# Three pairs of banks for h, one addition per operand, and other places for two sums in an attention and FFN kernel

## The chip, the cores and the metric

The kernel runs on one core of a Trainium2 chip. The metric is the device time of one execution in microseconds (us), from its start to its end. Three executions of the kernel before gave 823.32, 825.64 and 825.73 us, median 825.64. The profile was taken from an execution of 825.11 us.

## The reference

Attention within chunks of 64 tokens, then a feed-forward network with a quadratic activation. B is 8, H is 8, S is 576, D is 64, so x has 4608 rows of 512.

```python
# q, k, v: [B, H, S, D], cut into chunks of 64 along S
scores = scale * q_c @ k_c.transpose(-1, -2)
attn = exp(scores - max); attn = attn / (sum + 1e-9)
x = (attn @ v_c).reshape(...)            # 4608 x 512
h = x @ w_in                             # w_in 512 x 2048
g = where(h >= 1, h, where(h <= -1, 0, (h + 1) ** 2 / 4))
out = g @ w_out                          # w_out 2048 x 512
```

## The kernel before

**Tiles.** The 4608 tokens are nine tiles of 512. Tiles 0 to 2 go through the two products of the network directly: `ffn_in` (products on line 607) and `ffn_out` (line 643). Each float32 product is made of three, of a rounded high part and a low rest. Tiles 3 and 4, 5 and 6, 7 and 8 are three pairs, and a pair is treated together by the Strassen-Winograd scheme: seven products of combined blocks where eight would do it plainly. They are called pair 3, pair 5 and pair 7 here, by their first tile (the loop variable `t`).

**h of a pair.** The hidden dimension of a pair is cut into eight blocks, p = 0 to 7, and each block has seven products P1 to P7 (`product`, matmuls on line 899, six of 128x512 per product). P3(2) stands for product P3 of block 2. A block uses one pair of banks of the accumulation memory. Its first bank takes P1, P6, P5 and P3 one after the other, each added to what is there, and its second bank takes P2, then P7, then P4. Between the products the other engines read the bank. ACT and DVE are the scalar and the vector engine:

- after P1, ACT copies the bank to a snapshot ("note a", line 724); after P2, DVE adds bank and snapshot to h (line 920) and the activation follows (ACT lines 926 and 929, DVE line 930);
- after P6, ACT copies the bank to the other snapshot ("note u"); after P5, ACT copies it to h ("note h1") and DVE adds the bank of P7 to that ("add h1");
- P3 is activated straight from the bank (ACT line 926 and DVE line 930 read it); after P4, DVE adds the second snapshot ("add u") and the activation follows.

So P6 waits for note a, P5 for note u, P3 for note h1, P7 for the addition after P2, P4 for add h1, and the first product of a later block on the same banks waits for the activation of P3. The order of the products is `alternating`: block p and block p-1 are interleaved, so that between two products on one bank there stand products on others. In pairs 3 and 5 a burst of attention work (32 small products on lines 487 and 465, then maxima, eight exponentials on line 530 and transposes) is put in after every ninth product; pair 7 has none.

**Banks.** There are four sets. `h_banks` are two tiles of one bank each (ps_h in the trace, ps_h_141 and ps_h_142 in the program). `o_banks[:2]` are two tiles of one bank each (ps_o_139 and ps_o_140). `o_banks[2:]` are the two halves of ONE tile of two banks, made by `bank_pair("ps_o23")` (ps_o_137). `ps_a` serves the attention. In the trace ps_o stands for all three ps_o tiles. The framework puts the waits into the program: it follows readers and writers tile by tile.

**Out of a pair.** `both_out` makes the seven products of g with w_out, over all eight blocks (line 1114). Its `operand_of` splits the operands into high and low parts, and the table `after` says at which product the operand blocks are added in place by DVE.

**The order.** A planner (`Plan`) records every operation with a cost and what it reads and writes, and emits them engine by engine, each when its inputs are ready by the plan's own times, by its place in the code less a head start `ahead` (LATER is -60, that is later). The plan knows the two halves of `o_banks[2:]` as two banks.

**Sums and stores.** `keep_factor` (line 957) copies blocks of w_out to DRAM for the pairs: eight of P1 in tile 0, sixteen of P2 and P4 in tile 1. `combine_out` (DVE line 728, then four stores) makes sums of w_out, eight of them, the last two, 6 and 7, in pair 3 at P1(1) and P1(4). They work in one of two sets of temporaries: `tmp` (which tile 2's output also uses on its way to DRAM) or the `alt` tiles, chosen by `again`.

Of the kernel before, what the change touches and what calls it, by code (L numbers as in the profile page):

```python
# [12 lines left out]
ALU = mybir.AluOpType  # L13
# [120 lines left out]
def kernel(  # L134
# [36 lines left out]
    ALONE = 2  # L171
# [12 lines left out]
    def buffers(pool, name, n, dtype=F32):  # L184
        return [
            (f"{name}{i}", pool.tile([P, T], dtype, name=f"{name}{i}", tag=f"{name}{i}"))
            for i in range(n)
        ]
# [32 lines left out]
    o_banks = buffers(psum, "ps_o", 2) + [(f"ps_o{2 + b}", o_pair[:, b, :]) for b in range(2)]  # L221
    h_banks = buffers(psum, "ps_h", 2)
# [492 lines left out]
    def cols(n):  # L715
        return slice(n * QC, (n + 1) * QC)
# [5 lines left out]
    def act_copy(cost, out, src, reads, writes, ahead=0):  # L722
        plan.add(
            "act", cost, lambda: nc.scalar.copy(out=out(), in_=src()), reads, writes, ahead=ahead  # L724
        )

    def dve(cost, op, out, one, two, reads, writes, ahead=0):
        plan.add("dve", cost, lambda: nc.vector.tensor_tensor(  # L728
            out=out(), in0=one(), in1=two(), op=op
        ), reads, writes, port=True, ahead=ahead)  # L730

    def part(ap, n):
        return lambda: ap()[:, cols(n)]

    def plain(ap):
        return lambda: ap().bitcast(F32)
# [45 lines left out]
    def rounded(ap):  # L782
        return lambda: ap().bitcast(F32R)

    def stage_of(again):
        if again:
            some = [(f"alt{n}_{i}", part_of(f"alt{n}", i)) for n in range(2) for i in range(2)]
            return *some, [lambda n=n: held[f"alt{n}"] for n in range(2)]
        return *((key, fixed(ap)) for key, ap in tmp_bufs), [fixed(pair) for pair in tmp_pairs]
# [162 lines left out]
    def keep_factor(name, p):  # L952
        n, half = RAW[name]
        j = 2 * p + n

        def send():
            nc.gpsimd.dma_start(  # L957
                out=sums[name, p].bitcast(F32), in_=weight["wo", j][:, :, cols(half)].bitcast(F32)
            )

        plan.add("pool", 0.7, send, (f"wo{j}_0", f"wo{j}_1"), (f"sums_{name}_{p}",), lag=3.0,
                 moving=0.8, ahead=LATER)

    def combine_out(p, again=False):
        js = (2 * p, 2 * p + 1)
        keys = [[f"wo{j}_{n}" for n in range(2)] for j in js]
        (k1, w1), (k12, s12), (k2, w2), (k34, s34), pairs = stage_of(again)
        for j, ks, key, w in zip(js, keys, (k1, k2), (w1, w2)):
            dve(0.6, ALU.add, w, lambda j=j: weight["wo", j][:, 0, :].bitcast(F32),
                lambda j=j: weight["wo", j][:, 1, :].bitcast(F32), ks, (key,), ahead=LATER)  # L970
        a11, a21, a12, a22 = (part(w, n) for w in (w1, w2) for n in range(2))
        s1, s2, s3, s4 = (part(w, n) for w in (s12, s34) for n in range(2))
        dve(0.34, ALU.add, s1, a21, a22, (k1, k2), (k12,), ahead=LATER)
        dve(0.34, ALU.subtract, s2, s1, a11, (k1,), (k12,), ahead=LATER)
        dve(0.34, ALU.subtract, s3, a11, a21, (k1,), (k34,), ahead=LATER)
        dve(0.34, ALU.subtract, s4, a12, s2, (k2, k12), (k34,), ahead=LATER)
        for hkey, hi, key, ap in ((k1, w1, k12, s12), (k2, w2, k34, s34)):
            act_copy(0.52, rounded(hi), ap, (key,), (hkey,), ahead=LATER)
            dve(0.6, ALU.subtract, rounded(ap), ap, hi, (hkey,), (key,), ahead=LATER)
        for n, name in enumerate(SUMS):  # L980
            def send(n=n, name=name):
                nc.gpsimd.dma_start(
                    out=sums[name, p].bitcast(F32), in_=pairs[n // 2]()[:, :, cols(n % 2)]
                )

            plan.add("pool", 0.7, send, ((k1, k12), (k2, k34))[n // 2], (f"sums_{name}_{p}",),
                     lag=3.0, moving=0.8, ahead=LATER)

    def whole_last(p, name, banks):
        got = product(p, name, banks)  # L990
        if name == "P1":
            note(snap("a"), got)
        elif name == "P2":
            add(whole_h(0), got, snap("a"))
            activate(whole_h(0), blocks["eA", p])
        elif name == "P6":
            note(snap("u"), got)
        elif name == "P5":
            note(whole_h(1), got)
            add(whole_h(1), kept[p], whole_h(1))  # L1000
            activate(whole_h(1), blocks["oB", p])
        elif name == "P7":
            kept[p] = got
        elif name == "P3":
            activate(got, blocks["eB", p])
            (k1, a1), (k2, a2) = blocks["oB", p], blocks["eB", p]
            dve(0.6, ALU.subtract, lambda: now(a2), lambda: now(a1), lambda: now(a2), (k1,), (k2,))
        else:
            add(whole_h(0), got, snap("u"))
            activate(whole_h(0), blocks["oA", p])  # L1010
# [46 lines left out]
    def both_out(t, wide=(), then=None):  # L1057
# [9 lines left out]
        if not last:  # L1067
# [2 lines left out]
        alone = ("P1", "P2", "P7", "P5", "P3")  # L1070
        sources = {"P1": "eA", "P2": "oA", "P6": "eA", "P7": "eB", "P4": "oA", "P5": "eA", "P3": "oB"}
        after = {
            "P1": ((ALU.add, "eB", "eA", "eA"),),
            "P6": ((ALU.subtract, "oA", "eA", "oA"), (ALU.subtract, "oB", "eA", "eA")),
        }
        at = dict(blocks)

# [4 lines left out]
        def operand_of(name, p):  # L1082
            raws = {n: (at[n, p][0], lambda n=n: now(at[n, p][1])) for n in ("eA", "oA", "eB", "oB")}
            slot = both(f"x{one_of('slots', some.get(name, every))}")
            skey, ap = raws[sources[name]]
            (hkey, h), (lkey, l) = slot
            soon = 200 if name == "P1" and p < 2 else 0
            act_copy(0.52, h, ap, (skey,), (hkey,), ahead=soon)
            dve(0.6, ALU.subtract, l, ap, plain(h), (skey, hkey), (lkey,), ahead=soon)
            for op, *names in after.get(name, ()):  # L1090
                (k1, a1), (k2, a2), (okey, o) = (raws[n] for n in names)
                dve(0.6, op, o, a1, a2, (k1, k2), (okey,))
            return slot
# [216 lines left out]
    SUMS_AT = (0, 6, 12, 18, 20, 23)  # L1310
# [19 lines left out]
    for t in range(ALONE + 1):  # L1330
        for j in range(NF):
            step = (t - 1) * NF + j
            if t == 0:
                for what, g in SECOND.get(j, ()):
                    what(*divmod(NP + g, NP))
            elif step in SPREAD:
                n, m = SPREAD[step]
                if n is None and m == 2 * NP:
                    attn_turn(*AT[m])
                burst(n, m)  # L1340
                if m is not None and m + 1 <= 3 * NP + 1:
                    attn_turn(*AT[m + 1])
            ffn_in(t, j)
            prepare_next()
            m = t * NF + j - LAG
            if m >= 0:
                ffn_out(*divmod(m, NF))
            ffn_split(t, j)
            if step in WEIGHTS:
                combine_weights(WEIGHTS.index(step), step in AGAIN)  # L1350
            if step in SUMS_AT:
                combine_out(SUMS_AT.index(step), step in AGAIN)
            if t == 0 and j >= 8:
                keep_factor("P1", j - 8)
            elif t == 1:
                keep_factor("P2P4"[2 * (j % 2):][:2], j // 2)
            if t == ALONE and j < len(HANDED):
                hand_lot("wi", j, F32 if j < 2 else F32R, *HANDED[j])
                if j == 2:
                    hand_lot("wo", 0, F32R, "ring0")  # L1360
        if t:
            take_raws((first_raw, next_raw)[t - 1], t % 2)
# [17 lines left out]
    for t in range(ALONE + 1, NTILE, 2):  # L1380
        if t > ALONE + 1:
            move_blocks()
        for n, (p, name) in enumerate(alternating(0, NQ)):
            between(n)
            if t == ALONE + 1 and name == "P1":
                if p in (1, 4):
                    combine_out(len(SUMS_AT) + p // 4, p > 1)
                place_blocks(p)
            whole_last(p, name, o_banks[:2] if (p + (t > ALONE + 3)) % 2 else h_banks)
        if t < NTILE - 2:  # L1390
            raws = {(name, i): raw_of(t + 2, i, name) for i in range(2) for name in ("eA", "oA", "eB", "oB")}
            both_out(t, then=lambda raws=raws: pieces_of(raws))
        else:
            both_out(t, ('P1', 'P2', 'P6', 'P7', 'P4', 'P5'))
# [63 lines left out]
```

## Time and profile before

| | before |
|---|---|
| median of three executions | 825.64 us |
| the profiled execution | 825.11 us |
| its span, first to last instruction | 823.3 us |
| PE (matrix engine) busy | 808.5 us, 98% |
| DVE busy | 659.5 us, 80% |
| ACT busy | 539.0 us, 65% |
| POOL busy | 344.4 us, 42% |
| granted clock of PE | 1.000 |

The stretches of the span are: up to 18 us start-up, tile 0 to 104 us, tiles 1 and 2 to 326 us, then pair 3 (h to 408 us, out to 496), pair 5 (h to 580, out to 664) and pair 7 (h to 745, out to 819). PE is busy nearly all the time, so the reading goes by the few places where it isn't: the start of one product against the end of the product ahead, and what PE waited for there. A product group in the timeline lists its start, how long it lasted with its drain, and in square brackets the idle time before it with what ended it.

### The profile page before, as it was taken

What the parts mean: (1) busy time and instruction counts of PE and PEld (TensorE: products, weight loads), DVE (VectorE), ACT (ScalarE), POOL (GpSimd) and SP (SyncE); (2) the same over time, 40 slices, a digit from 0 to 9 for tenths busy, and PEclk for the clock granted to TensorE, in tenths of its full rate; (3) what the DMA queues carried; (4) which work ended last, traced back from release to release, by engine and by line L of the source; (5) the groups of instructions that cost most, each with busy time, mean ns of one, the idle gap of its engine ahead of it and who ended that gap; (6) DMA issues with size and microseconds to landing.
All of it is one profiled execution on the core that took longest, in us unless ns stands there. A gap on an engine that the chain in (4) does not pass through costs nothing.

```text
span 823.3 us, 18510 instructions
## 1 busy us (share of the span) xinstructions
PE 808.5 (98%) x6464; PEld 693.5 (84%) x6464; DVE 659.5 (80%) x1143; ACT 539.0 (65%) x1295; POOL 344.4 (42%) x606
## 2 busy tenths in 40 slices
PE   8999999999999999999999999999999999999998
PEld 7877778888888788778899998788999988888887
DVE  5989998778899986678899785787994855589963
ACT  5789876455667675687885445888844546686440
POOL 2133343345355463365454333555333334433330
PEclk9999999999999999999999999999999999999999
DMA  9999955666798897899999678987665776666673
GB/s 219 259 315 292 295 137 153 201 193 183 189 267 229 217 267 189 244 288 262 251 238 269 181 228 241 248 244 210 189 202 182 230 219 193 193 194 188 202 212 112
DMA packets 245356, 181.61 MB, mean 221 GB/s; under 512 B 192656, under 2 KB 210576, under 8 KB 245264
## 3 DMA queue, kind: packets, MB, share of 16 engines
q0 software_dynamic: 40640, 122.72, 47.7%
q1 hardware_dynamic: 202512, 57.18, 30.5%
q8 instruction: 52, 0.85, 0.4%
q10 hardware_dynamic: 2112, 0.52, 0.3%
q14 instruction: 40, 0.33, 0.2%
HBM read 133.17 MB, written 38.80 MB: 209 GB/s over the span
## 4 chain that ended last, share of the span: by engine, by line
PE 64%; DVE 12%; DMA 9%; ACT 5%; issue 5%; SPq 3%; POOL 2%; DVEq 0%; ACTq 0%; POOLq 0%
PE ps_o L1114 19%; PE ps_o L899 11%; PE ps_h L899 11%; PE ps_h L1114 8%; PE ps_o L643 5%; PE ps_h L607 5%; PE ps_a L1114 3%; DMA aT<-x 2%; DVE tmp L728 2%; DMA sums_P<-parts 2%; ACT e L530 1%; DVE new_wi L728 1%; DVE r L618 1%; DMA combos<-tmp 1%; PE ps_a L487 1%
## 5 line engine op out<-in xcount | busy, mean ns | idle before, releaser
L724 ACT CAST new_wi<-new_wi 128x512 fp32r<-128x512 f32 x154 | 94.4, 628 | 66.3 <-PE ps_o L1114 33.7
L728 DVE TENSOR_TENSOR new_wi<-new_wi,new_wi 128x512 fp32r<-128x512 f32 (+2 forms) x192 | 123.5, 676 | 15.6 <-ACT new_wi L724 15.2
L607 PE MATMUL ps_h<-xh,parts 128*128 128x512 f32 x384 | 129.9, 398 | 2.9 <-DVE parts L350 1.7
L643 PE MATMUL ps_o<-parts,gh 128*128 128x512 f32 x384 | 118.5, 390 | 0.0
L607 PEld LDWEIGHTS ps_h<-xh,parts 128*128 128x128 f32 x384 | 71.9, 188 | 19.8 <-DVE parts L350 2.6
L643 PEld LDWEIGHTS ps_o<-parts,gh 128*128 128x128 f32 x384 | 71.9, 188 | 15.0
L643 PE MATMUL ps_o<-parts,gl 128*128 128x512 f32 x192 | 74.8, 390 | 1.0 <-DVE gl L628 1.0
L562 POOL DMA_DIRECT2D aT<-e x96 | 48.5, 520 | 42.0 <-PE ps_h L607 11.1
L930 DVE SCALAR_TENSOR_TENSOR new_wi<-h,new_wi 128x512 f32<-128x512 f32 x62 | 42.1, 684 | 27.7 <-ACT new_wi L929 27.7
L530 ACT ACTIVATE e<-ps_a,mx 128x64 f32<-128x64 f32 x168 | 50.2, 328 | 10.0 <-DVE mx L526 5.9
L929 ACT ACTIVATE new_wi<-new_wi 128x512 f32<-128x512 f32 x84 | 51.6, 634 | 1.1
L926 ACT ACTIVATE new_wi<-h 128x512 f32<-128x512 f32 x62 | 39.6, 641 | 16.1 <-DVE h L920 15.9
L607 PE MATMUL ps_h<-x_parts,parts 128*128 128x512 f32 x128 | 50.0, 391 | 0.0
L626 ACT CAST gh<-r 128x512 fp32r<-128x512 f32 x48 | 30.0, 625 | 29.1 <-DVE r L618 22.2
L643 PEld LDWEIGHTS ps_o<-parts,gl 128*128 128x128 f32 x192 | 36.0, 188 | 8.9 <-DVE gl L628 1.4
L957 POOL DMA_DIRECT2D sums_P<-parts x24 | 17.8, 788 | 57.7 <-DVE parts L350 57.5
L628 DVE TENSOR_TENSOR gl<-r,gh 128x512 fp32r<-128x512 f32 x48 | 32.8, 685 | 7.8 <-ACT gh L626 7.1
L618 DVE SCALAR_TENSOR_TENSOR r<-ps_h,r 128x512 f32<-128x512 f32 x48 | 32.5, 681 | 7.2 <-ACT r L617 7.1
L728 DVE TENSOR_TENSOR new_wi<-new_wi 128x512 f32<-128x512 f32 (+2 forms) x60 | 37.4, 635 | 0.3
L530 ACT ACTIVATION_READ_ACCUMULATOR e<-ps_a,mx 128x1 f32 x168 | 37.1, 221 | 0.0
L1114 PE MATMUL ps_o<-new_wo,new_wi 128*128 128x256 f32 (+1 forms) x244 | 34.8, 292 | 0.0
L1114 PE MATMUL ps_o<-ring_gh,new_wi 128*128 128x256 f32 (+1 forms) x244 | 34.6, 292 | 0.0
(264 smaller groups left out, 2155.0 us busy)
## 6 DMA issues: line engine op xcount, KB each, us to landing
ring_gh<-combos POOLq DMA_DIRECT2D x36, 256.0 KB, 4.3
new_wo<-sums_P POOLq DMA_DIRECT2D x36, 256.0 KB, 3.3
new_wi<-combos POOLq DMA_DIRECT2D x34, 256.0 KB, 4.1
ring_gl<-combos POOLq DMA_DIRECT2D x34, 256.0 KB, 3.8
ring_r<-sums_P POOLq DMA_DIRECT2D x34, 256.0 KB, 3.2
new_wi<-sums_P POOLq DMA_DIRECT2D x34, 256.0 KB, 3.3
words<-in_moe_w_in_dram SPq DMA_DIRECT2D x16, 512.0 KB, 7.1
words<-in_moe_w_out_dram SPq DMA_DIRECT2D x16, 512.0 KB, 6.0
```

The lines of the kernel that those rows point to most:

```text
L530: nc.scalar.activation(out=e3[:, n, :], in_=sc[:, n // 4, n % 4, :], func=AF.Exp, bias=mx[:, n, :], scale=SCALE, accum_out=sm[:, n, :],)
L562: queues[queue].dma_start(out=aT[b:b + Q, to], in_=x[a:a + Q, of])
L607: nc.tensor.matmul(out=ps, lhsT=weight["wi", j][:, half, kc * P:(kc + 1) * P], rhs=x, start=(kc == 0 and i == 0), stop=(kc == KC - 1 and i ...
L618: plan.add("dve", 0.6, lambda: nc.vector.scalar_tensor_tensor(out=r, in0=ps, scalar=1.0, in1=r, op0=ALU.max, op1=ALU.min), (pkey,), (rkey,))
L643: nc.tensor.matmul(out=acc, lhsT=x[:, cols], rhs=weight["wo", j][:, half, :], start=(j == 0 and i == 0), stop=(j == NF - 1 and i == 2),)
L724: "act", cost, lambda: nc.scalar.copy(out=out(), in_=src()), reads, writes, ahead=ahead
L728: plan.add("dve", cost, lambda: nc.vector.tensor_tensor(out=out(), in0=one(), in1=two(), op=op), reads, writes, port=True, ahead=ahead)
L899: nc.tensor.matmul(out=ps, lhsT=w()[:, at:at + P], rhs=y(), start=name in FRESH and i == 0 and k == 0, stop=i == 1 and k == 2, skip_group_ ...
L926: plan.add("act", 0.52, lambda: nc.scalar.activation(out=now(r), in_=h(), func=AF.Relu, bias=0.5, scale=0.5), (hkey,), (rkey,), ahead=50)
L929: plan.add("act", 0.52, lambda: nc.scalar.square(out=now(r), in_=now(r)), (), (rkey,), ahead=50)
L930: plan.add("dve", 0.6, lambda: nc.vector.scalar_tensor_tensor(out=now(r), in0=h(), scalar=1.0, in1=now(r), op0=ALU.max, op1=ALU.min), (hke ...
L1114: nc.tensor.matmul(out=into, lhsT=x()[:, block], rhs=factor, start=first and k == 0, stop=p == NQ - 1 and k == len(steps) - 1, skip_group_ ...
```

## The change

Four things. Block p of a pair takes the bank sets in turn by p % 3, h banks, `o_banks[:2]`, `o_banks[2:]`, where it took the first two in turn. The in-place additions of `both_out` stand one at each of P2, P6 and P7, where P1 had one and P6 two. Sum 6 is made in the `alt` tiles and sum 7 in `tmp`, the other way round than before. The P1 stores of `keep_factor` are recorded in tile 1 with those of P2 and P4, none in tile 0.

```diff
--- before.py
+++ after.py
@@ -1070,8 +1070,8 @@
         alone = ("P1", "P2", "P7", "P5", "P3")
         sources = {"P1": "eA", "P2": "oA", "P6": "eA", "P7": "eB", "P4": "oA", "P5": "eA", "P3": "oB"}
         after = {
-            "P1": ((ALU.add, "eB", "eA", "eA"),),
-            "P6": ((ALU.subtract, "oA", "eA", "oA"), (ALU.subtract, "oB", "eA", "eA")),
+            "P2": (ALU.add, "eB", "eA", "eA"), "P6": (ALU.subtract, "oA", "eA", "oA"),
+            "P7": (ALU.subtract, "oB", "eA", "eA"),
         }
         at = dict(blocks)
 
@@ -1087,7 +1087,8 @@
             soon = 200 if name == "P1" and p < 2 else 0
             act_copy(0.52, h, ap, (skey,), (hkey,), ahead=soon)
             dve(0.6, ALU.subtract, l, ap, plain(h), (skey, hkey), (lkey,), ahead=soon)
-            for op, *names in after.get(name, ()):
+            if name in after:
+                op, *names = after[name]
                 (k1, a1), (k2, a2), (okey, o) = (raws[n] for n in names)
                 dve(0.6, op, o, a1, a2, (k1, k2), (okey,))
             return slot
@@ -1350,10 +1351,9 @@
                 combine_weights(WEIGHTS.index(step), step in AGAIN)
             if step in SUMS_AT:
                 combine_out(SUMS_AT.index(step), step in AGAIN)
-            if t == 0 and j >= 8:
-                keep_factor("P1", j - 8)
-            elif t == 1:
-                keep_factor("P2P4"[2 * (j % 2):][:2], j // 2)
+            if t == 1:
+                for name in ("P4",) if j % 2 else ("P1", "P2"):
+                    keep_factor(name, j // 2)
             if t == ALONE and j < len(HANDED):
                 hand_lot("wi", j, F32 if j < 2 else F32R, *HANDED[j])
                 if j == 2:
@@ -1384,9 +1384,9 @@
             between(n)
             if t == ALONE + 1 and name == "P1":
                 if p in (1, 4):
-                    combine_out(len(SUMS_AT) + p // 4, p > 1)
+                    combine_out(len(SUMS_AT) + p // 4, p == 1)
                 place_blocks(p)
-            whole_last(p, name, o_banks[:2] if (p + (t > ALONE + 3)) % 2 else h_banks)
+            whole_last(p, name, (h_banks, o_banks[:2], o_banks[2:])[p % 3])
         if t < NTILE - 2:
             raws = {(name, i): raw_of(t + 2, i, name) for i in range(2) for name in ("eA", "oA", "eB", "oB")}
             both_out(t, then=lambda raws=raws: pieces_of(raws))
```

What this does to the order of PE is shown at one place, the h products of pair 7, from P5(2) on. The operand names are ring buffers; ps_o_139 and ps_o_140 are `o_banks[:2]`, ps_o_137 is both halves of `o_banks[2:]`, ps_h_141 and ps_h_142 are the h banks. Waits on Activation are for ACT, those on DMASW for loads. Before:

```order
L899 MATMUL ps_o_139<-new_wi_5_2891,new_wi_9_3187 128x512 [waits DMASW7_49,Activation_49]
L899 MATMUL ps_o_139<-new_wi_5_2891,new_wi_9_3187 128x512 x2
L899 MATMUL ps_o_139<-new_wi_8_3118,new_wi_9_3187 128x512 x3
L899 MATMUL ps_h_142<-low_2_7440,ring_gh_3704 128x512 [waits DMASW0_49,DVE_49]
L899 MATMUL ps_h_142<-low_3_7441,ring_gh_3704 128x512
L899 MATMUL ps_h_142<-low_2_7440,ring_gh_3704 128x512
L899 MATMUL ps_h_142<-new_wi_6_2965,ring_gh_3704 128x512 x3
L899 MATMUL ps_o_139<-new_wi_3_2703,ring_gh_3733 128x512 [waits DMASW1_49,Activation_49]
L899 MATMUL ps_o_139<-new_wi_3_2703,ring_gh_3733 128x512 x2
L899 MATMUL ps_o_139<-new_wi_7_3031,ring_gh_3733 128x512 x3
```

The products are P5(2), P2(3), P3(2); the last waits for ACT. After, the same three:

```order
L899 MATMUL ps_o_137<-new_wi_5_2891,new_wi_9_3187 128x512 [waits DMASW7_49,Activation_49]
L899 MATMUL ps_o_137<-new_wi_5_2891,new_wi_9_3187 128x512 x2
L899 MATMUL ps_o_137<-new_wi_8_3118,new_wi_9_3187 128x512 x3
L899 MATMUL ps_h_142<-low_2_7440,ring_gh_3706 128x512 [waits DMASW0_49]
L899 MATMUL ps_h_142<-low_3_7441,ring_gh_3706 128x512
L899 MATMUL ps_h_142<-low_2_7440,ring_gh_3706 128x512
L899 MATMUL ps_h_142<-new_wi_6_2965,ring_gh_3706 128x512 x3
L899 MATMUL ps_o_137<-new_wi_3_2703,ring_gh_3735 128x512 [waits DMASW1_49,DVE_49]
L899 MATMUL ps_o_137<-new_wi_3_2703,ring_gh_3735 128x512 x2
L899 MATMUL ps_o_137<-new_wi_7_3031,ring_gh_3735 128x512 x3
```

The order of the products is the same; P3(2) now waits for DVE (add h1, which reads the other half of ps_o_137), and P2(3) no longer waits for DVE.

On ACT, in pair 3, from the activation of P3(2) to the exponentials of the next burst. Line 926 with a bank as its input is the first step of that activation, the copy on line 724 to snaps is note u of block 3. Before:

```order
L926 ACTIVATE new_wi_13_3491<-h 128x512 [waits DVE_49]
L926 ACTIVATE new_wi_12_3471<-ps_h_141 128x512 [waits PE_49]
L929 ACTIVATE new_wi_13_3491<-new_wi_13_3491 128x512 [waits Activation_49]
L929 ACTIVATE new_wi_12_3471<-new_wi_12_3471 128x512 [waits Activation_49]
L926 ACTIVATE new_wi_12_3471<-h 128x512 [waits DVE_49]
L724 COPY raw_2436<-ps_a 128x2x4x64 [waits DVE_49]
L724 COPY snaps<-ps_o_139 128x512 [waits PE_49]
L929 ACTIVATE new_wi_12_3471<-new_wi_12_3471 128x512 [waits Activation_49]
```

After:

```order
L926 ACTIVATE new_wi_13_3503<-h 128x512 [waits DVE_49]
L926 ACTIVATE new_wi_12_3471<-ps_o_137 128x512 [waits PE_49]
L929 ACTIVATE new_wi_13_3503<-new_wi_13_3503 128x512 [waits Activation_49]
L929 ACTIVATE new_wi_12_3471<-new_wi_12_3471 128x512 [waits Activation_49]
L926 ACTIVATE new_wi_12_3471<-h 128x512 [waits DVE_49]
L724 COPY raw_2436<-ps_a 128x2x4x64 [waits DVE_49]
L724 COPY snaps<-ps_h_141 128x512 [waits PE_49]
L929 ACTIVATE new_wi_12_3471<-new_wi_12_3471 128x512 [waits Activation_49]
```

The instructions stand in the same order; the second one waits for the last product written to ps_o_137 ahead of it. That is P4(2) and no longer P3(2), since the program has P4(2) on the same tile by then.

On POOL, the stores of `keep_factor` around 91 us, as a difference (minus is before, plus is after):

```order
 L957 DMA sums_P_3_159<-parts_1081 256x1x256
 L562 DMA aT_78<-e_77 32x256 x8
+L957 DMA sums_P_3_183<-parts_1081 256x1x256
 L957 DMA sums_P_4_152<-parts_1141 256x1x256
-L957 DMA sums_P_3_183<-parts_1081 256x1x256
 L957 DMA sums_P_4_160<-parts_1184 256x1x256
```

Two of the 24 stores change places; the others stand where they stood.

## Rows read from the trace of the kernel before

**Rows 1.** The page: busy time, share of the span and instructions per engine.

```profile
PE 808.5 (98%) x6464; PEld 693.5 (84%) x6464; DVE 659.5 (80%) x1143; ACT 539.0 (65%) x1295; POOL 344.4 (42%) x606
```

**Rows 2.** Windows: length, busy PE, PEld, DVE, ACT, POOL, clock, DMA share.

```profile
18.00:104.00 86.00, 81.74 (x750) 65.53 (x741) 81.68 (x120) 72.60 (x151) 28.67 (x44) 1.00 1.01 288
...
408.00:496.00 88.00, 88.00 (x822) 86.68 (x821) 78.19 (x134) 54.08 (x125) 38.17 (x72) 1.00 0.82 230
...
664.00:745.00 81.00, 81.00 (x365) 67.09 (x364) 50.49 (x79) 55.83 (x102) 32.04 (x60) 1.00 0.66 199
745.00:819.00 74.00, 74.00 (x451) 65.68 (x450) 55.84 (x101) 30.25 (x53) 23.36 (x44) 1.00 0.62 181
```

**Rows 3.** Timeline of PE: late h products (start, length, idle before and its end).

```profile
338.95 1.65 PE L899 MATMUL ps_h<-new_wi,ring_r 128*128 128x512 f32 x6 [1.47 <-DVE h L920]
...
355.00 0.96 PE L899 MATMUL ps_o<-xl,ring_r 128*128 128x512 f32 x3 [0.59 <-DVE new_wi L930]
...
514.16 0.97 PE L899 MATMUL ps_h<-low,new_wi 128*128 128x512 f32 x3 [0.28 <-DVE new_wi L930]
...
529.26 1.52 PE L899 MATMUL ps_o<-new_wi,ring_gh 128*128 128x512 f32 x6
530.82 1.62 PE L899 MATMUL ps_o<-new_wi,ring_gl 128*128 128x512 f32 x6
```

**Rows 4.** Timeline: DVE's first addition of sum 6, in pair 3.

```profile
333.12 0.69 DVE L728 TENSOR_TENSOR tmp<-parts 128x512 f32<-128x512 f32 x1 [1.89 <-DMA out_dram<-tmp]
```

**Rows 5.** Timeline, tile 2's end: ACT and DVE copy one half each of ps_o23.

```profile
326.67 0.59 ACT L659 COPY tmp<-ps_o 128x512 f32<-128x512 f32 x1 [1.45 <-PE ps_o L643]
...
327.29 0.69 DVE L657 COPY tmp<-ps_o 128x512 f32<-128x512 f32 x1 [1.29 <-ACT tmp L659]
```

**Rows 6.** Timeline in pair 7: PE after P5(2), note h1(2), add h1(2).

```profile
691.01 0.84 PE L899 MATMUL ps_h<-low,ring_gh 128*128 128x512 f32 x3
691.21 0.59 ACT L724 COPY h<-ps_o 128x512 f32<-128x512 f32 x1 [0.77 <-PE ps_o L899]
...
691.83 0.69 DVE L920 TENSOR_TENSOR h<-ps_o,h 128x512 f32<-128x512 f32 x1 [1.18 <-ACT h L724]
```

**Rows 7.** Timeline of PE in pair 3: P4(2), P2(4), P3(3).

```profile
360.59 0.84 PE L899 MATMUL ps_h<-new_wi,new_wi 128*128 128x512 f32 x3
...
368.71 0.84 PE L899 MATMUL ps_h<-xl,ring_gl 128*128 128x512 f32 x3
...
370.38 2.34 PE L899 MATMUL ps_o<-new_wi,ring_r 128*128 128x512 f32 x9 [0.15 <-ACT h L724]
```

**Rows 8.** Timeline of ACT there: activation of P3(2), first exponential, notes a(4), h1(3).

```profile
361.14 0.58 ACT L926 ACTIVATE new_wi<-ps_h 128x512 f32<-128x512 f32 x1
361.62 1.14 ACT L929 ACTIVATE new_wi<-new_wi 128x512 f32<-128x512 f32 x2
...
366.88 0.32 ACT L530 ACTIVATE e<-ps_a,mx 128x64 f32<-128x64 f32 x1
...
369.20 0.64 ACT L724 COPY snaps<-ps_h 128x512 f32<-128x512 f32 x1
369.67 0.67 ACT L724 COPY h<-ps_o 128x512 f32<-128x512 f32 x1
```

**Rows 9.** Timeline in pair 3: addition after P2(5), add h1(4); PE at P6(5), P4(4).

```profile
381.63 0.69 DVE L920 TENSOR_TENSOR h<-ps_o,snaps 128x512 f32<-128x512 f32 x1 [1.75 <-PE ps_o L899]
...
382.56 0.64 DVE L920 TENSOR_TENSOR h<-ps_h,h 128x512 f32<-128x512 f32 x1
...
381.36 1.52 PE L899 MATMUL ps_o<-new_wi,ring_gl 128*128 128x512 f32 x6
...
384.08 1.52 PE L899 MATMUL ps_h<-new_wi,ring_gl 128*128 128x512 f32 x6
```

**Rows 10.** Timeline in pair 3: ACT's cast of a sum; the product after P5(1).

```profile
345.42 0.67 ACT L724 CAST tmp<-tmp 128x512 fp32r<-128x512 f32 x1
...
346.08 0.86 PE L899 MATMUL ps_h<-xl,new_wo 128*128 128x512 f32 x3
```

## The prediction

> **What bounds the kernel now.** I read the page first: PE is busy 98% of the span [rows 1], at a clock of 1.00 in every window [rows 2]. So a change pays only where PE stands still, or costs where it makes PE stand still. I then went through PE's timeline by the starts of products: two 128x512 products of six follow each other at 1.36 us (529.26 and, undisturbed, 530.62), whatever drain the records show. The windows tell which stretches have nothing to win: PE is full in the output parts of the pairs and in all of h of pair 7 [rows 2]. The late starts of h are few [rows 3]: P4(0) of pair 3 at 338.95, P1(3) at 355.00, P1(2) of pair 5 at 514.16, P7(3) at 530.82, and P3(3) of pair 3 at 370.38 [rows 7]. To the idle time in brackets belong 0.16 us of drain that the next product would have overlapped (1.52 less 1.36), and about 0.12 us because the first product after a stop runs slower (1.65 against 1.52). So P1(3) lost 0.59 + 0.16 + 0.12 = 0.87 us, P4(0) 1.75 and P3(3) 0.43. P1(2) of pair 5 follows a burst, whose restart costs its 0.12 anyway, and 0.35 us are put down to the wait; P7(3) lost some 0.27; two smaller late starts of pair 5 together 0.23, and one of pair 3 0.11.
>
> **What the third set of banks removes.** P1(3) and P1(2) waited for the activation of a P3 that had the same first bank two blocks earlier. With three sets in turn that activation lies a block further back, and P7(3)'s wait for the addition after P2(3) moves by a product. I take all of these as gone: 0.87 and 0.11 us in pair 3, 0.35 + 0.27 + 0.23 = 0.85 us in pair 5. Pair 7 has none to remove.
>
> **What it adds.** The third set is one tile of two banks, and waits are made by tile. The trace of before has one place where this shows: at the end of tile 2 ACT copies one half of ps_o23 and DVE the other; DVE, idle, starts at 327.29, with ACT's copy (326.67 + 0.59 = 327.26) as what released it [rows 5], though they read different banks into different buffers. So each block with p % 3 = 2, blocks 2 and 5, gets waits that its data don't need. The order of the changed program shows them; PE pays for them as follows.
>
> - P3(2) waits for add h1, where note h1 sufficed. In pair 7 note h1(2) starts at 691.21, add h1(2) at 691.83 and ends at 692.52; P3(2) could start 0.04 later (as 370.38 after 369.67 + 0.67 [rows 7, 8]), at 692.56. It was due at 691.01 + 1.36 = 692.37 [rows 6]. So 0.19 + 0.12 = 0.31 us, wherever only P2(3) lies between: P3(2) in all three pairs, and P3(5) in pair 7. In pairs 3 and 5 a burst hides P3(5)'s. Four times 0.31 is 1.24 us.
> - The activation of P3(2) reads the tile that P4(2) writes next, so it waits for P4(2)'s end. ACT runs in order, and its exponentials and note h1(3) stand behind it. Before, in pair 3, the activation started at 361.14 [rows 8]; P4(2) ends at 360.59 + 1.36 = 361.95 [rows 7], and a reader starts 0.20 later (691.21 after 691.01 [rows 6]), so it moves to 362.15, by 1.01 us. The chain from there to note h1(3) has no slack: P3(3) comes at 370.38 + 1.01 = 371.39, due at 368.71 + 1.36 = 370.07. That is 1.32 + 0.12 = 1.44 us in place of 0.43. In pair 5 the order is the same, but P3(3) was not late there, so between 0 and 1.44; I take 0.72.
> - The addition after P2(5) waits for P6(5)'s end, since P6(5) writes the same tile by then. DVE is in order, add h1(4) stands behind it, and P4(4) waits for that. Before, the addition started at 381.63; now at 381.36 + 1.36 + 0.20 = 382.92, 1.29 later. Add h1(4) then ends at 382.56 + 0.64 + 1.29 = 384.49, P4(4) starts at 384.53, due at 384.08 [rows 9]: 0.45 + 0.12 = 0.57 us, in pairs 3 and 5.
> - The activation of P3(5) waits for P4(5). Behind it stand the squares (about 1.1), the exponentials (369.20 - 366.88 = 2.32) and note u(6) (0.64) [rows 8]: 0.20 + 0.48 + 1.1 + 2.32 + 0.64 + 0.04 = 4.78 us after P4(5). P5(6) is due three products later, 4.08. So 0.70 + 0.12 = 0.8 us, in pairs 3 and 5.
> - P2(2) in pair 3 waits for note a(2), which stands behind ACT's cast of a sum. The cast starts at 345.42 [rows 10] and ACT steps every 0.5, so the note ends at 345.93 + 0.64 = 346.57. P2(2) takes the place of the product that started at 346.08: 0.53 + 0.12 = 0.65 us. From 0 (if the cast is earlier) to 1.
> - In pair 5 P2(2) comes ahead of note a(2), which so waits for P2(2)'s end; note u(1) stands behind it on ACT, and P5(1), the next product, waits for note u(1): 0.20 + 0.47 + 0.67 + 0.04 + 0.12 = 1.5 us [rows 8].
>
> The Trainium skill ("PSUM — Partial Sum Buffer", section "PSUM bank collisions raise a hardware error") asks to guard this memory by bank and quadrant, and says that accesses to different banks run clean. By that the waits above are more than the chip needs, and with waits by bank the sum would hold only the removed 2.26 us; rows 5 show that this program waits by tile.
>
> **The other three parts.** The additions of the output part: DVE does the same number, two instead of three operations at P6. PE has no stop there to remove (88.00 of 88.00 busy, 74.00 of 74.00 [rows 2]), and DVE has 10 to 18 us of room in these windows. Zero; a loss would need DVE to fall behind, which the even spread makes less likely. The sums: P4(0)'s 1.75 us come from DVE, which at 333.12 had waited 1.89 for tile 2's stores to leave `tmp` [rows 4], with add h1(0) queued behind it on DVE. Sum 7's first additions now stand at the same place in DVE's order on the same `tmp`, so the stop stays: zero, at best a gain of 1.75. The stores: only two of 24 change places on POOL, since the planner emitted the others late already. Tile 0's window has full DMA (1.01) and 86.00 - 81.74 = 4.26 us without PE [rows 2]; that bounds a gain, and with the transfers where they were I take zero.
>
> **The sum.** Pair 3: 0.65 + 0.31 + 1.44 + 0.57 + 0.8 = 3.77 added, 0.87 + 0.43 + 0.11 = 1.41 removed, +2.36. Pair 5: 1.5 + 0.31 + 0.72 + 0.57 + 0.8 = 3.90 added, 0.85 removed, +3.05. Pair 7: 0.62. Together +6.0 on the profiled execution's 825.11 us (span 823.3 and 1.8 around it): 831.1. That execution lies 0.5 below the median of the three.
>
> **The rivals.** (a) *The rotation pays.* The waits by tile are covered by other stops or loads, P3(2) starts on time, and only the removals count: 825.11 - 0.98 - 0.43 - 0.85 = 822.85; with P4(0)'s stop gone too, 821.1. Its deciding point is P3(2) in pair 7: if it starts 1.36 after P2(3), this case holds. For it: ACT and DVE are idle a third and a fifth of the span [rows 1]. The Trainium skill ("Perfetto Trace Analysis", section "Matmuls") says that independent groups should rotate through different banks so that emptying one overlaps the next group; by that rule the time is this case's. Against it: pair 7 has no bursts and no slack between note and product, and the waits are in the program. (b) *Only the short waits cost.* The chains over ACT and DVE behind the bursts (P3(3), P4(4), P5(6)) are absorbed by slack that I don't see, and P3(3) keeps its 0.43: 1.24 + 0.65 + 1.5 - 0.98 - 0.85 = +1.6, 826.7. (c) *The change of sums removes P4(0)'s stop* while the waits cost what I say: 831.1 - 1.75 = 829.3. (d) *It does not do what it says*: the stores stay in tile 0. This is in my forecast already.
>
> **How the numbers follow.** A measurement here tells 0.3%, 2.5 us, from no change, that is 823.2 to 828.1. My forecast, with (c) and with pair 5's P3(3) at either end (830.4 to 831.9), gets 0.72, all slower. Case (b) gets 0.17, within 0.3%. Case (a) gets 0.11, at or below the lower edge, counted as 0.10 faster and 0.01 the same. The range leaves out (a): from 824.5, below (b) by the spread of the three runs, to 833.0, where P2(2) and P3(3) are at their upper ends and the three runs' spread is added.
>
> **What would show it.** In the changed profile: P3(2) in pair 7 late by 0.3 with DVE's line 920 as releaser, and P3(5) as well; P5(1) of pair 5 late by 1.5, behind ACT's line 724; P3(3) of pair 3 late by 1.4; P4(0) still late by 1.75; output parts with PE full. It would be wrong if PE showed no stops at blocks 2 and 5, if P4(0) started on time, or if DVE fell behind in an output part.

## The result and the profile after

The changed kernel takes 834.07 us, median of four executions (832.23 to 835.04), against 825.65 for the kernel before: a ratio of 1.0106, 95% interval 1.008 to 1.0132. It is slower, as forecast, and slower than forecast: 831.1 was said and up to 833.0 was allowed. Its profiled execution took 833.37 us, 8.26 more than the one of before, and the span grew by as much, from 823.3 to 831.6.

The page of the changed kernel, the same two parts as before (busy time with share of the span and instructions; the granted clock in 40 slices):

```profile
PE 813.0 (98%) x6464; PEld 693.7 (83%) x6464; DVE 658.4 (79%) x1143; ACT 538.3 (65%) x1295; POOL 343.9 (41%) x606
...
PEclk9999999999999999999999999999999999999999
```

DVE, ACT and POOL do the work they did [rows 1], and the clock is full. PE's share of 98% tells nothing: the answer is in what PE waited for. The list of PE's waits in the changed kernel (us in total, times, longest), those of the h products (line 899):

```profile
PE ps_h L899 <- DVE h L920: 2.1, 1, 2.1
...
PE ps_h L899 <- ACT h L724: 1.7, 2, 0.9
PE ps_o L899 <- ACT snaps L724: 1.5, 2, 1.2
...
PE ps_h L899 <- ACT snaps L724: 1.0, 2, 0.5
PE ps_o L899 <- DVE h L920: 0.7, 2, 0.4
...
PE ps_o L899 <- ACT h L724: 0.6, 2, 0.3
```

The wait of P1(3) for the activation on DVE line 930 [rows 3] is no longer in the list; in its place stand notes of ACT (line 724, into h and into the snapshots) and additions of DVE (line 920). The list leaves out what the drain of the product ahead covers, so the shortest stops can only be seen in the timeline. The first place is the same as in rows 6, pair 7 from P5(2) on (start, length, engine, line, and idle before):

```profile
698.22 0.84 PE L899 MATMUL ps_h<-low,ring_gh 128*128 128x512 f32 x3
698.42 0.59 ACT L724 COPY h<-ps_o 128x512 f32<-128x512 f32 x1 [0.46 <-PE ps_o L899]
...
699.04 0.69 DVE L920 TENSOR_TENSOR h<-ps_o,h 128x512 f32<-128x512 f32 x1 [0.83 <-ACT h L724]
...
699.79 1.23 PEld L899 LDWEIGHTS ps_o<-new_wi,ring_gh 128*128 128x128 f32 x6 [0.47 <-DVE h L920]
699.79 1.66 PE L899 MATMUL ps_o<-new_wi,ring_gh 128*128 128x512 f32 x6
```

P3(2) was due at 698.22 + 1.36 = 699.58 and starts at 699.79, 0.06 after add h1 ended at 699.73. The row of the matmuls carries no bracket, since the drain of P2(3) covers the idle time; the row of the weight loads names DVE line 920. The product group lasts 1.66 where it lasted 1.52, so the restart costs 0.14; 0.11 of that falls on its first matmul, and this is what the sums here count. So 0.21 + 0.11 = 0.32 us.

The other late products of the changed kernel, in pairs 3 and 5. In order: P2(2), P5(3), P3(3), P4(4), P5(1) of pair 5, P3(3) of pair 5, P5(6) of pair 5, P3(7) of pair 5:

```profile
346.77 0.97 PE L899 MATMUL ps_o<-xl,new_wi 128*128 128x512 f32 x3 [0.38 <-ACT snaps L724]
...
367.76 1.67 PE L899 MATMUL ps_h<-new_wi,ring_gl 128*128 128x512 f32 x6
...
371.63 2.11 PE L899 MATMUL ps_h<-new_wi,ring_r 128*128 128x512 f32 x8 [0.81 <-ACT h L724]
...
385.86 1.43 PE L899 MATMUL ps_o<-new_wi,ring_gl 128*128 128x512 f32 x5 [0.36 <-DVE h L920]
...
519.48 1.20 PE L899 MATMUL ps_o<-new_wi,ring_gh 128*128 128x512 f32 x4 [1.16 <-ACT snaps L724]
...
544.40 1.88 PE L899 MATMUL ps_h<-new_wi,new_wo 128*128 128x512 f32 x7 [0.85 <-ACT h L724]
...
574.37 1.65 PE L899 MATMUL ps_h<-new_wi,ring_r 128*128 128x512 f32 x6 [0.49 <-ACT snaps L724]
...
587.32 1.89 PE L899 MATMUL ps_o<-new_wi,ring_gl 128*128 128x512 f32 x7 [0.30 <-ACT h L724]
```

Each bracket plus 0.16 of drain and 0.11 of restart is what the stop took. P5(3) has no bracket: it was due at 367.56, 1.36 after P1(4), and starts 0.20 later. P4(0) of pair 3 is late as before [rows 3], by more, and its DVE row shows why: the first addition of sum 7 stands where that of sum 6 stood [rows 4] and waits for the same stores.

```profile
332.81 0.69 DVE L728 TENSOR_TENSOR tmp<-parts 128x512 f32<-128x512 f32 x1 [2.06 <-DMA out_dram<-tmp]
335.75 0.69 DVE L728 TENSOR_TENSOR tmp<-parts 128x512 f32<-128x512 f32 x1 [2.24 <-DMA out_dram<-tmp]
...
338.38 0.65 DVE L920 TENSOR_TENSOR h<-ps_h,h 128x512 f32<-128x512 f32 x1
339.09 1.65 PE L899 MATMUL ps_h<-new_wi,ring_r 128*128 128x512 f32 x6 [2.09 <-DVE h L920]
```

### The profile page after: what moved, and what is told of

It is laid out like the page before. It is cut to its first block, busy times and chain, and to the rows that moved or that the text cites. A ratio compares the mean times of both kernels' runs of the same rounds, so it can differ in the third digit from the quotient of the medians.

```text
span 831.6 us, 18504 instructions
## 1 busy us (share of the span) xinstructions
PE 813.0 (98%) x6464; PEld 693.7 (83%) x6464; DVE 658.4 (79%) x1143; ACT 538.3 (65%) x1295; POOL 343.9 (41%) x606
## 4 chain that ended last, share of the span: by engine, by line
PE 73%; DMA 10%; ACT 5%; DVE 5%; SPq 4%; issue 3%; POOL 0%; ACTq 0%; DVEq 0%; POOLq 0%
PE ps_o L1115 18%; PE ps_o L899 13%; PE ps_o L643 10%; PE ps_h L607 10%; PE ps_h L1115 8%; PE ps_h L899 7%; PE ps_a L1115 3%; DMA k_sb<-in_k_dram 3%; DMA words<-in_moe_w_in_dram 2%; PE ps_a L487 2%; ACT e L530 2%; PE ps_a L465 1%; SPq L382 1%; DMA v_sb<-in_v_dram 1%; ACT x L530 1%
```

## The experiments

Each run was compared with the kernel before on the same chip; its median differs from chip to chip (824.7 to 826.3 us), so the ratios count.

**Which part of the change.** First the third set of banks alone, then all the rest without it.

```diff
 # e1_banks, against the kernel before
-            whole_last(p, name, o_banks[:2] if (p + (t > ALONE + 3)) % 2 else h_banks)
+            whole_last(p, name, (h_banks, o_banks[:2], o_banks[2:])[p % 3])
```

> The kernel before with the first part of the change alone: h over three pairs of banks, p % 3. Theory A (the waits by tile of the third pair, plus the planner's other order, are the whole loss): the time of the changed kernel, 833 to 835 us, with the same late products, P3(2) in all three pairs, P3(3), P4(4), P5(6), P3(7). Theory B (a share of the loss comes from the additions, the sums or the stores): below 832 us. If A holds, the difference to the changed kernel is under 1 us.

```diff
 # e2_rest, against the changed kernel
-            whole_last(p, name, (h_banks, o_banks[:2], o_banks[2:])[p % 3])
+            whole_last(p, name, o_banks[:2] if (p + (t > ALONE + 3)) % 2 else h_banks)
```

> The changed kernel with the first part undone: h over two pairs of banks as before, the additions, sums and stores as changed. Theory A: 825 to 826.5 us, the same as before. Theory B: 827 us or more, with new stops of PE in the output parts or in tile 0.

The first took 833.89 us, ratio 1.0112 (1.0095 to 1.013); the second 824.77, ratio 0.9996 (0.9982 to 1.0009). So the whole loss is the third set's, and the additions, sums and stores are worth nothing that can be measured. At the output parts no stop appeared: in the second kernel the window of pair 3's output reads

```profile
412.00:500.00 88.00, 88.00 (x813) 86.27 (x812) 76.11 (x130) 51.44 (x115) 37.47 (x72) 1.00 0.80 231
```

(length, then busy PE, PEld, DVE, ACT, POOL, the clock, DMA), as full as in rows 2.

**The tile or the rotation.** The third pair as two tiles of one bank. What used both banks in one instruction is done in two halves, in tile 0's attention and at the end (these edits are left out below); the planner's keys, and so the order of the h products, stay. The same split is put into the kernel before as the control.

```diff
 # e3_split_after, against the changed kernel; e5_split_before, the same against the kernel before
-    o_pair, a_pair = bank_pair("ps_o23"), bank_pair("ps_a")
-    o_banks = buffers(psum, "ps_o", 2) + [(f"ps_o{2 + b}", o_pair[:, b, :]) for b in range(2)]
+    a_pair = bank_pair("ps_a")
+    o_banks = buffers(psum, "ps_o", 4)
...
+    o_pair = Two(o_banks[2][1], o_banks[3][1])
```

> The changed kernel with the third pair of banks as two tiles of one bank each, so that waits are made bank by bank; the few instructions that used both banks at once (softmax and split of every second turn in tile 0, the evacuation of the last output part) are done in two halves. The planner sees the same keys, so its order of the h products stays. Theory A: the stops at blocks 2 and 5 (together 9.0 us in the changed kernel's trace: P2(2), P5(1), P3(2), P5(3), P3(3), P4(4), P5(6), P3(5)) go, the late P3(7) of pairs 3 and 5 (0.57 us each) stays: 824.5 to 826.5 us. Theory C (three pairs in turn cost by the other order itself, whatever the tiles): 831 us or more.

> The control of the run above: the kernel before with the same split of the tile and the same halved instructions, h over two pairs. Both theories: 825.5 to 827 us, what the halved instructions cost in tile 0 and at the end, 0 to 1 us. The difference between the run above and this one is the worth of three pairs in turn without waits by tile: A -1.5 to +0.5 us (2.3 us of stops removed, 1.4 us of P3(7) and P5(7) added), C +5 us or more.

The changed kernel with the split took 823.46 us, ratio 0.9986 (0.9975 to 0.9997), a little less than I expected, since P3(7), which I took to stay late, came nearly on time; the control 824.85, ratio 1.0005 (0.9995 to 1.0016). So the split alone changes nothing, the same split takes some 10 us off the changed kernel, and then three sets in turn are worth about 1.4 us. The control also settles the reading of rows 5: there ACT's copy starts at 326.00 and DVE's at 326.68, each released by PE, and neither waits for the other any more. The same place of pair 7 in the split kernel (its lines are 40 further down: 939 is 899, 960 is 920, 764 is 724):

```profile
689.57 0.84 PE L939 MATMUL ps_h<-low,ring_gh 128*128 128x512 f32 x3
...
690.39 0.69 DVE L960 TENSOR_TENSOR h<-ps_o,h 128x512 f32<-128x512 f32 x1 [1.45 <-ACT h L764]
690.93 1.52 PE L939 MATMUL ps_o<-new_wi,ring_gh 128*128 128x512 f32 x6
```

P3(2) starts at 689.57 + 1.36 = 690.93, while add h1 is still reading the other bank (until 691.08). In the changed kernel it waited for that very addition. The Trainium skill ("PSUM — Partial Sum Buffer", section "PSUM bank collisions raise a hardware error") asks for guards by bank and quadrant. The split kernel runs with waits by bank, and the waits by tile, the part in excess, cost the difference between 1.0106 and 0.9986. Of P3(3), late by 0.43 in pair 3 of the kernel before, 0.41 us is there in pair 3 and now in pair 5 too.

**The tile without a third set.** The kernel before, two sets in turn, the second of which is the shared tile.

```diff
 # e4_shared_two, against the kernel before
-            whole_last(p, name, o_banks[:2] if (p + (t > ALONE + 3)) % 2 else h_banks)
+            whole_last(p, name, o_banks[2:] if (p + (t > ALONE + 3)) % 2 else h_banks)
```

> The kernel before with one word changed: of its two pairs of banks for h, the second is the shared tile (both halves of ps_o23) in place of the two separate tiles. The planner's order of every engine is that of the kernel before; only what the waits are tied to differs. Theory A (waits by tile cost, whatever the rotation): in pair 7 four blocks lie on the shared tile, and P3(0), P3(2), P3(4), P3(6) each start 0.3 us late, 1.2 us in all; with the chains of pairs 3 and 5 the time is 831 to 840 us. Theory C (the third set or its order costs, not the tile): 824 to 826 us and no late P3 in pair 7.

It took 858.57 us, ratio 1.0398 (1.0367 to 1.0429), far more than I said. The run isn't as clean as I had written: the order of PE isn't that of the kernel before, since the output parts begin on `o_banks[2:]`, so block 7 and the first output product now share banks (the latter waits 2.6 us in pair 3 and again in pair 5, for line 930). In pair 7 the stops are those that were forecast, and more; shown are P6(0) and P7(0) at its start, then PE from P2(1) to P1(2):

```profile
694.81 1.65 PE L899 MATMUL ps_o<-new_wi,ring_gl 128*128 128x512 f32 x6 [0.68 <-ACT snaps L724]
697.32 1.65 PE L899 MATMUL ps_o<-new_wi,ring_gl 128*128 128x512 f32 x6 [0.85 <-DVE h L920]
...
702.21 0.84 PE L899 MATMUL ps_h<-new_wi,new_wo 128*128 128x512 f32 x3
703.09 1.67 PE L899 MATMUL ps_o<-new_wi,new_wo 128*128 128x512 f32 x6
...
707.35 1.52 PE L899 MATMUL ps_h<-new_wi,ring_gh 128*128 128x512 f32 x6
709.28 0.96 PE L899 MATMUL ps_o<-low,ring_gh 128*128 128x512 f32 x3 [0.41 <-DVE h L920]
```

P3(0) starts at 703.09 where 702.21 + 0.68 = 702.89 was due, and P3(2) and P3(4) are late by the same 0.2, without any third set. P1(2) is late by another 0.57: it takes the banks that block 0 has just left, and waits for add u(0) there. P6(0) and P7(0) are late by 0.84 and 1.01, with a note and an addition as releasers. From its first product to the end pair 7 takes 165.6 us, 6.0 more than before, and there is no stop at its output. So the shared tile costs without the rotation. Of the 33 us in all, these 6.0 go with waits on the shared tile, and the stops of the first output product in pairs 3 and 5 take some 5.8; how the rest divides was not taken apart.

**Block by block.** Only block 2, then only block 5, on the shared tile.

```diff
 # e8_block2, against the changed kernel (e9_block5: (0, 1, 0, 1, 0, 2, 0, 1))
-            whole_last(p, name, (h_banks, o_banks[:2], o_banks[2:])[p % 3])
+            whole_last(p, name, (h_banks, o_banks[:2], o_banks[2:])[(0, 1, 2, 0, 1, 0, 1, 0)[p]])
```

> The changed kernel with only block 2 on the third pair (one tile of two banks); blocks 0 to 7 take the sets 0, 1, 2, 0, 1, 0, 1, 0. Theory A with stops that belong to their block: P2(2), P5(1), P3(2), P5(3) and P3(3) stay (5.9 us in the changed kernel's trace), P4(4), P5(6), P3(7) and P3(5) (4.5 us) go: 829 to 831 us. If P3(7)'s lateness in pairs 3 and 5 has nothing to do with block 5's waits, it stays here.

> The counterpart: only block 5 on the third pair, the sets being 0, 1, 0, 1, 0, 2, 0, 1. P4(4), P5(6), P3(7) and P3(5) stay (4.5 us), the stops of block 2 go, and P1(3) (0.87 us) and P3(3) (0.43 us) of pair 3 are late again as in the kernel before: 828.5 to 831 us. P3(7) is late if block 5's waits make it so.

They took 829.94 us, ratio 1.0043 (1.0025 to 1.0062), and 831.45, ratio 1.0068 (1.0042 to 1.0094). With block 2 alone P2(2), P5(1), P3(2), P5(3) and P3(3) are late as in the changed kernel, and P3(7) is on time; in pair 3 it follows the output product ahead of it at 410.87 + 1.43 = 412.30:

```profile
410.87 1.59 PE L1115 MATMUL ps_o<-ring_gl,new_wi 128*128 128x256 f32 x12
412.30 1.55 PE L899 MATMUL ps_h<-new_wi,new_wi 128*128 128x512 f32 x6
```

With block 5 alone P3(7) is late, by 0.28 us and the restart (415.90, due at 414.19 + 1.43 = 415.62):

```profile
397.02 2.35 PE L899 MATMUL ps_o<-new_wi,new_wi 128*128 128x512 f32 x9 [1.10 <-DVE h L920]
...
414.19 1.59 PE L1115 MATMUL ps_o<-ring_gl,new_wi 128*128 128x256 f32 x12
415.90 2.33 PE L899 MATMUL ps_o<-new_wi,ring_gh 128*128 128x512 f32 x9
```

So P3(7) belongs to block 5. The first of these rows is P3(5), late by 1.37 (1.20 in pair 5): in this order no burst lies over it, as one does in the changed kernel. These two stops were not in my bounds, and block 5 alone came out a little above them.

**The stop at P4(0).** Both late sums in the alt tiles, in the split kernel and in the kernel before; then, in the split kernel, sum 7 in tmp but held back until after P5(2).

```diff
 # e6_split_after_alt, against e3_split_after; e7_before_alt has the same in the kernel before
-                    combine_out(len(SUMS_AT) + p // 4, p == 1)
+                    combine_out(len(SUMS_AT) + p // 4, True)
 # e10_split_after_late, against e3_split_after; the first two additions read (*ks, *after)
-                    combine_out(len(SUMS_AT) + p // 4, p == 1)
+                    combine_out(len(SUMS_AT) + p // 4, p == 1, (blocks["oB", 2][0],) if p == 4 else ())
```

> The changed kernel with the third pair split into two tiles, and both late sums (6 and 7) in the alt tiles, none in tmp. If P4(0)'s stop in pair 3 (1.54 us and 0.11 at the restart, in the split kernel's trace) comes from the sum that waits for tile 2's stores to leave tmp, it goes: 823.5 less 1.65, about 821.8 us. If the second sum in the same tiles makes a new wait of DVE, or add h1(0) is late for another reason, 823 to 824 us.

> The kernel before with both late sums in the alt tiles. By the same reasoning P4(0)'s stop of 1.75 us goes: 1.7 us below the kernel before, ratio 0.998. If it is late for another reason: no change.

> The changed kernel with the third pair split into two tiles, and sum 7 (in tmp) held back in the planner's order until after the product P5(2) of pair 3, so that its first addition no longer stands ahead of add h1(0) on DVE. If P4(0)'s stop comes from that place in DVE's order, it goes without a new one: 823.5 less 1.65, about 821.8 us, ratio to before 0.996 to 0.997. If the stop comes back elsewhere, as with both sums in the alt tiles (where DVE's second sum stood ahead of the last evacuations of tile 2 and P1(0) stopped for 2.0 us): 823 us or more.

The two with alt tiles are slower, where I expected them to be faster, 828.66 us (ratio 1.0036, 1.0021 to 1.005) and 828.71 (1.0049, 1.0024 to 1.0074). P4(0) is on time, but the sum's additions now come earlier on DVE, ahead of tile 2's last evacuations, and P1(0) stops. P1(1) stops as well, for a load of its factor. In the kernel before with both sums in alt, at P1(0) and P1(1), and then the windows around P1(0) (the seventh figure is the clock):

```profile
319.53 0.65 DVE L618 SCALAR_TENSOR_TENSOR r<-ps_h,r 128x512 f32<-128x512 f32 x1
...
320.24 1.19 PE L899 MATMUL ps_h<-xl,new_wo 128*128 128x512 f32 x3 [1.89 <-DVE r L618]
...
333.89 0.93 PE L899 MATMUL ps_o<-xl,ring_gh 128*128 128x512 f32 x3 [0.88 <-DMA ring_gh<-combos]
...
312.00:320.00 8.00, 6.35 (x29) 4.92 (x27) 7.96 (x17) 7.30 (x25) 0.00 (x0) 1.00 0.49 83
320.00:324.00 4.00, 3.76 (x10) 3.00 (x11) 3.52 (x7) 2.25 (x4) 3.10 (x6) 0.60 0.26 66
324.00:330.00 6.00, 6.00 (x27) 4.91 (x27) 1.11 (x2) 1.17 (x2) 5.47 (x10) 0.98 0.88 282
```

DVE is full ahead of the stop (7.96 of 8.00), and a clock of 0.60 behind it makes it dearer. The stop at P1(1) costs another 1.04 and the restart; in the split kernel with alt tiles it is 1.49. This profile is of an execution of 825.18 us, at the low end of the twelve (825.08 to 835.04), so it shows where PE stops and not all of what the median loses. Holding the sum back does what was wanted: 823.02 us, ratio 0.9958 (0.9942 to 0.9974). P4(0) starts right behind the product ahead of it, and add h1(0) was done in time:

```profile
337.87 0.69 DVE L960 TENSOR_TENSOR h<-ps_h,h 128x512 f32<-128x512 f32 x1 [0.25 <-ACT h L764]
338.40 1.52 PE L939 MATMUL ps_h<-new_wi,ring_gl 128*128 128x512 f32 x6
...
339.76 1.52 PE L939 MATMUL ps_h<-new_wi,ring_r 128*128 128x512 f32 x6
```

This is the fastest kernel of the study, 0.4% below the kernel before.

## Why the prediction was right in kind and short in size

**The mechanism: right.** The waits by tile of the third pair are the loss: the third set alone brings it (1.0112), and two tiles in its place take it away (0.9986). Where the prediction speaks of a chain on ACT without slack, behind P3(2), the trace has one over two engines: ACT waits 1.44 and 0.57 us for DVE in it, and it is 5.77 us long where it was 5.74, so it passes the delay on whole. The deciding point of rival (a), P3(2) in pair 7, fell as the forecast said. Rival (a) itself became true in the split kernel: waits by bank, three sets in turn, 1.4 us gained where the removed stops were counted at 2.3.

**The terms.** Late time of each product with its restart (0.11, its first matmul), from the starts in the timeline of the changed kernel:

| place | said | measured |
|---|---|---|
| P2(2), pair 3 | 0.65 | 0.66 |
| P3(2), three pairs, and P3(5), pair 7 | 1.24 | 4 x 0.32 = 1.27 |
| P5(3) and P3(3), pair 3 | 1.44 | 0.31 + 1.08 = 1.39 |
| P5(3) and P3(3), pair 5 | 0.72 | 0.31 + 1.12 = 1.43 |
| P4(4), pairs 3 and 5 | 1.14 | 2 x 0.64 = 1.27 |
| P5(6), pairs 3 and 5 | 1.6 | 2 x 0.77 = 1.53 |
| P5(1), pair 5 | 1.5 | 1.43 |
| P3(7), pairs 3 and 5 | 0 | 0.56 + 0.57 = 1.13 |
| P5(7), pair 7 | 0 | 0.22 |
| removed, pairs 3 and 5 | -2.26 | -2.26, as counted |
| all up to P4(0) of pair 3, this included | 0 | +0.14 |

The sum is 6.0 said and 8.2 measured, against 8.3 of the span. Every late product whose time was worked out from rows held within 0.15 us, P2(2) too, for which 0 to 1 was allowed: ACT's cast stands where it stood, at 345.55 against 345.42 [rows 10].

**The step that failed** is the list of places, and one choice. First, P3(7). I followed each new wait to the next product that needs the delayed bank and stopped there. But the delay goes on, by way of DVE. In pair 3 of the changed kernel the exponentials behind the late activation of P3(5) hold up DVE until 401.07 (line 547). From there DVE waits for no other engine until it has made the maxima of the last burst (line 521, at 408.66), and ACT, idle for 0.31 us, waits for these. Then come the last burst's exponentials on ACT at 411.51, note h1(7) at 413.83, and P3(7), due at 414.06, at 414.51:

```profile
401.07 0.17 DVE L547 TENSOR_SCALAR sm<-sm 128x8 f32<-128x8 f32 x1 [0.40 <-ACT e L530]
...
408.66 0.68 DVE L521 TENSOR_REDUCE mx<-ps_a 128x8 f32<-128x512 f32 x1
...
411.51 0.31 ACT L530 ACTIVATE e<-ps_a,mx 128x64 f32<-128x64 f32 x1
...
413.83 0.63 ACT L724 COPY h<-ps_o 128x512 f32<-128x512 f32 x1
...
412.63 1.60 PE L1115 MATMUL ps_o<-ring_gl,new_wi 128*128 128x256 f32 x12
414.51 1.66 PE L899 MATMUL ps_o<-new_wi,ring_gh 128*128 128x512 f32 x6 [0.28 <-ACT h L724]
```

The split kernel has the same two rows of DVE (its lines 571 and 545) the same 7.6 us apart:

```profile
397.05 0.17 DVE L571 TENSOR_SCALAR sm<-sm 128x8 f32<-128x8 f32 x1 [0.40 <-ACT e L554]
...
404.65 0.69 DVE L545 TENSOR_REDUCE mx<-ps_a 128x8 f32<-128x512 f32 x1
```

But there P3(7) is due at 410.53, 13.48 us after the first row, and comes 0.06 late; in the changed kernel it is due 12.99 after it, 0.49 sooner, and comes 0.45 late. That the stop belongs to block 5 is shown by this and by the two runs block by block. Second, P3(3) of pair 5: "P3(3) was not late there, so between 0 and 1.44; I take 0.72". The slack I allowed for isn't there: with P5(3) the late time is 1.43 us in pair 5, as in pair 3 (1.39). That it was on time before says only that the chain just fitted. In pair 3 part of the delay already shows at P5(3), a stop that I had folded into P3(3).

**The range.** Its upper end, 833.0, had P2(2) and P3(3) at their upper ends and nothing for stops that were not on the list. These (P3(7) and P5(7)) made 1.35 us, more than any error in a listed term, and the measured 834.07 lies 1.1 us above.

**The other parts: right.** The additions and the stores changed nothing, and the sums left P4(0) late, at DVE's same place: e2_rest came out at 0.9996. In the profiled execution P4(0) is late by 2.25 + 0.11, not 1.75, but P1(0) comes on time, where it lost 0.54 before, and the two cancel but for 0.07. That they do is chance: in the profiles of e1_banks and e5_split_before P1(0) is on time too, and P4(0) waits only 1.31 and 1.29 us there, against 1.47 before and 2.09 in the changed kernel. So the length of this stop varies by at least 0.8 us from profile to profile.

## What to carry to other kernels

Before banks are used in a new turn, look up what the waits are tied to: two banks in one tile are one bank to the program, and the planner that thinks them two will place readers and products side by side that in fact queue. When a wait is added on an engine that works in order, follow its queue and the queues of the engines that wait for it to the end, until the delay is seen to be absorbed, and not only to the first product that comes late. Idle time on the first engine is no proof: here ACT was idle three times on the way (0.43, 0.41 and 0.31 us), and the delay went on over DVE. And a product that starts on time may have no slack: take the full shift for it unless a row shows how long the note had been ready.

## What the runs showed that was not expected

In the kernel before with both sums in alt, PE stopped for about 2.05 us at 318 us, and the clock of the next window was 0.60: products of 128x512 followed at 0.43 us in place of 0.227 for about nine of them, so that the stop cost another 1.7 us or so. This is the lower of the two levels (1.2 GHz) for part of that window, full speed again after 324 us (0.98). In the changed kernel PE stopped for 2.25 us ahead of P4(0), and the clock stayed at its upper level. The kernel with the shared tile and no third set shows both after stops of one length: before the first output product of pair 3 and of pair 5 PE waited 2.61 us each time, and of the windows that follow the first has a clock of 0.63, a part of it at the lower level, the second 1.00:

```profile
427.80:431.80 4.00, 3.98 (x22) 3.98 (x23) 3.66 (x8) 4.00 (x16) 0.54 (x1) 0.63 1.05 166
...
610.50:614.50 4.00, 4.00 (x33) 4.00 (x34) 3.97 (x7) 3.69 (x8) 1.07 (x2) 1.00 0.17 39
```

So the length of the stop alone does not decide it. What does was not tried.
